# First block in two halves, smaller first weight pieces, an earlier w_out load, and transposes ahead of the first store, in a gated recurrence with a maxout layer

## The chip, the cores and the metric

The kernel runs on one core of a Trainium2 chip. The metric is the device time of one execution in microseconds (us), as the median of several runs. The engines are TensorE (PE; its weight loads are PEld), VectorE (DVE), ScalarE (ACT), GpSimd (POOL) and SyncE (SP). DMAs are issued from SP's and POOL's queues, and two from ACT's at the very end.

## What is computed

The first stage is a gated linear recurrence along the sequence, the second a maxout layer with two weight matrices and an output matrix (4 batches of 6144 positions, 256 features, 1024 hidden):

```
sig = 1 / (1 + exp(-f_logit))
f = lower_bound + (1 - lower_bound) * sig ;  i = 1 - f
for t in range(S):
    h = f[:, t] * h + i[:, t] * x[:, t] ;  y[:, t] = h
h1 = y @ w1 ;  h2 = y @ w2
out = maximum(h1, h2) @ w_out
```

## The kernel before

**Algebra.** With u = sigmoid(-f_logit) the decay is 1 - (1 - lower_bound) * u, and the drive is u * x; the factor (1 - lower_bound) of the drive is left out of the recurrence and put into the weights. As max(h1, h2) = h1 + relu(h2 - h1), the output is y @ (w1 @ w_out) + relu(y @ (w2 - w1)) @ w_out. So the kernel makes `wd` (w2 - w1, scaled, bf16) and `w13` (w1 @ w_out, scaled, bf16) once. `wd` comes from the fp32 difference `wdf`; for `w13` the fp32 w1 is transposed on PE to `w1T`.

**Blocks and chunks.** A block is 512 positions of one batch, 48 in all; features lie on the partitions, in KC = 2 halves of 128. Loads are by chunk: the first four chunks are one block each, the rest two. Chunk 0 is loaded as fp32 by SP and cast by DVE (L95 to L102). Chunks 1 to 3 are loaded with a cast by POOL (L113) and, like chunk 0, turned by PE transposes into PSUM (`turn_steps`, L133). From chunk 4 on POOL casts them into one of two scratch tensors in DRAM (L106), and SP's transposing DMA brings them in (`cross`, L123).

**A block's work.** `gate` (L161): ACT's sigmoid, giving u. `scan_steps` (L175): DVE's drive (v), two decays (ff), two scans (y), each scan starting from the last column of the block before. `first_layer(j, fc)` (L312): for one of FC = 8 hidden blocks, two matmuls with `wd` into the PSUM tile dT (three buffers) and ACT's relu into rt. `second_layer(j, slot)` (L330): the 40 matmuls of the block with w13 and w_out, five a slot, into psO (three buffers); DVE copies psO to osb at L366, SP stores osb at L369 (four osb buffers).

**Order.** The schedule is written by hand: each engine runs its instructions in the order of the text, held only by the data. In the text of the start (L384 to L439) stand: chunk 0's loads, four weight pieces of 512 KB (`fetch_w`, w2 then w1 for each half of the hidden blocks), 8 transposes of an identity, block 0's transposes and recurrence, POOL's wait on the first w1 piece and its load of w_out (L400), a second POOL wait on the second w2 piece, then chunks 1 to 5. Then `turn_w1` (eight fp32 transposes of w1, L288), `make_wd` in steps of two hidden blocks (one DVE subtraction and two ACT scalings each), block 0's first layers in between, `keep_w1T` (copies to w1T, L295), `make_w13`, then block 1's transposes and recurrence, block 0's second layer, block 2's transposes, block 1's first layer, block 2's recurrence, block 3's transposes and gate. A loop over j from 2 then runs first_layer(j) and second_layer(j - 1) side by side, one slot of each in turn, and block j + 1's scan steps among them; for j = 2 all of second_layer(1) comes first. `ahead` issues crossings and fetches a set number of blocks early; in SP's queue the first store stands ahead of the first crossing.

Of the kernel before, what the change touches and what calls it, by code (L numbers as in the profile page):

```python
# [9 lines left out]
FP32 = mybir.dt.float32  # L10
# [8 lines left out]
def kernel(  # L19
# [34 lines left out]
    NCHUNK = len(chunks)  # L54

    def by_xbar(c, s):
        return c >= (4, 4)[s]

    const = ctx.enter_context(tc.tile_pool(name="const", bufs=1))
    wpool = ctx.enter_context(tc.tile_pool(name="wpool", bufs=1))  # L60
# [30 lines left out]
    def fetch(c):  # L91
        b, t0, nt, _ = chunks[c]
        for s in range(2):
            src = srcs[s][b, t0 : t0 + nt, :]
            if c == 0:  # L95
                raw = const.tile([P, nt // P, D], FP32, name=("f0", "x0")[s])
                nc.sync.dma_start(  # L97
                    out=raw[:], in_=src.rearrange("(p i) d -> p i d", p=P)
                )
                nat = natpool.tile([P, CH // P, D], BF16, name=("fn", "xn")[s])  # L100
                nc.vector.tensor_copy(out=nat[:, 0 : nt // P, :], in_=raw[:])  # L101
                held[c, s] = nat  # L102
            elif by_xbar(c, s):
                scr = scratch[s][uses[s] % NSCR]
                uses[s] += 1
                nc.gpsimd.dma_start(  # L106
                    out=scr[0:nt, :].rearrange("(p i) d -> p (i d)", p=P),
                    in_=src.rearrange("(p i) d -> p (i d)", p=P),
                )
                held[c, s] = scr  # L110
            else:
                nat = natpool.tile([P, CH // P, D], BF16, name=("fn", "xn")[s])
                nc.gpsimd.dma_start(  # L113
                    out=nat[:, 0 : nt // P, :].rearrange(
                        "p (k i) d -> p k (i d)", i=TB // P
                    ),
                    in_=src.rearrange(
                        "(k p i) d -> p k (i d)", p=P, i=TB // P
                    ),
                )  # L120
                held[c, s] = nat

    def cross(c):  # L123
        nt = chunks[c][2]
# [28 lines left out]
    def turn(steps):  # L153
        for dst, src in steps:
            nc.tensor.transpose(dst, src, ident[:])  # L155
# [5 lines left out]
    def gate(j):  # L161
        nb = blocks[j][2]
        u = midpool.tile([P, KC, TB], BF16, name="u")
        src = turned[j, 0]
        nc.scalar.activation(  # L165
            out=like(u[:, :, 0:nb], src), in_=src, func=AF.Sigmoid, scale=-1.0
        )
        us[j] = u

    def like(t, src):  # L170
        if len(src.shape) == 3:
            return t
        return t.rearrange("p k (m i) -> p k m i", m=P)

    def scan_steps(j):  # L175
        b, t0, nb, c, o = blocks[j]
        u = us[j]
        ff = midpool.tile([P, KC, TB], BF16, name="ff")
        v = midpool.tile([P, KC, TB], BF16, name="v")
        y = ypool.tile([P, KC, TB], BF16, name="y")  # L180
        ys[j] = y

        def decay(h):
            nc.vector.tensor_scalar(  # L184
                out=ff[:, h, 0:nb],
                in0=u[:, h, 0:nb],
                scalar1=nom[:, h : h + 1],
                scalar2=1.0,
                op0=ALU.mult,
                op1=ALU.add,  # L190
            )

        def drive():
            src = turned[j, 1]
            nc.vector.tensor_tensor(  # L195
                out=like(v[:, :, 0:nb], src),
                in0=like(u[:, :, 0:nb], src),
                in1=src,
                op=ALU.mult,
            )  # L200

        def scan(h):
            if t0 == 0:
                init = 0.0
            else:
                pn = blocks[j - 1][2]
                init = ys[j - 1][:, h, pn - 1 : pn]
            nc.vector.tensor_tensor_scan(  # L208
                out=y[:, h, 0:nb],
                data0=ff[:, h, 0:nb],  # L210
                data1=v[:, h, 0:nb],
                initial=init,
                op0=ALU.mult,
                op1=ALU.add,
            )

        return [
            drive,
            lambda: decay(0),
            lambda: decay(1),  # L220
            lambda: scan(0),
            lambda: scan(1),
        ]

    def recurrence(j):
        gate(j)
        for step in scan_steps(j):
            step()
# [19 lines left out]
    def half(w, g):  # L248
        return w[g][:].rearrange("p kc (m q) -> p kc q m", q=NQ)
# [14 lines left out]
    def pool_waits(t):  # L264
        nc.gpsimd.tensor_copy(out=waited[:], in_=t)

    def pair(w, k):
        return w[:, :, 2 * k * P : 2 * k * P + 2 * P].rearrange(
            "p kc (q m) -> p kc q m", q=2
        )  # L270

    def make_wd(k):
        g, r = divmod(k, NQ // 2)
        qs = slice(2 * r, 2 * r + 2)
        nc.vector.tensor_tensor(  # L275
            out=pair(wdf, k), in0=half(w2n, g)[:, :, qs], in1=half(w1n, g)[:, :, qs],
            op=ALU.subtract,
        )
        cols = slice(2 * k * P, 2 * k * P + 2 * P)
        for kc in range(KC):  # L280
            nc.scalar.mul(wd[:, kc, cols], wdf[:, kc, cols], om[:, kc : kc + 1])  # L281

    def turn_w1(k):
        g, r = divmod(k, NQ // 2)
# [98 lines left out]
    with tc.manual_schedule():  # L383
        nc.sync.dma_start(out=lbc[:], in_=lower_bound.rearrange("(h p) -> p h", p=P))  # L384
        nc.vector.tensor_copy(out=ident[:], in_=ident_f[:])
        nc.vector.tensor_scalar(
            out=om[:], in0=lbc[:], scalar1=-1.0, scalar2=1.0, op0=ALU.mult, op1=ALU.add
        )
        nc.vector.tensor_scalar_add(out=nom[:], in0=lbc[:], scalar1=-1.0)
        fetch(0)  # L390
        for g in range(NG):
            fetch_w(g)
        nc.scalar.activation(out=warm[:], in_=om[:, 0:1], func=AF.Sigmoid)
        wt = ps_d.tile([P, TB], BF16, name="dT")
        for q in range(8):
            nc.tensor.transpose(wt[:, 0:P], ident[:], ident[:])
        turn(turn_steps(0))
        recurrence(0)
        pool_waits(w1n[0][:, 0, 0:1])
        nc.gpsimd.dma_start(  # L400
            out=wob[:].rearrange("p (g q) c -> p g (q c)", g=NG),
            in_=moe_w_out.rearrange("(g p q) c -> p g (q c)", g=NG, q=NQ),
        )
        pool_waits(w2n[1][:, 0, 0:1])
        fetch(1)
        fetch(2)
        done["fetch"] = 3
        ahead("fetch", fetch, LEAD_FETCH)
        pts = [turn_w1(0), turn_w1(1)]
        make_wd(0)  # L410
        make_wd(1)
        for fc in range(0, 2):
            first_layer(0, fc)
        keep_w1T(0, pts[0])
        make_wd(2)
        for fc in range(2, 4):
            first_layer(0, fc)
        make_wd(3)
        keep_w1T(1, pts[1])
        pts = [turn_w1(2), turn_w1(3)]  # L420
        for fc in range(4, 6):
            first_layer(0, fc)
        keep_w1T(2, pts[0])
        for fc in range(6, 8):
            first_layer(0, fc)
        keep_w1T(3, pts[1])
        make_w13()
        turn(turn_steps(1))
        recurrence(1)
        for fc in range(FC):  # L430
            second_layer(0, fc)
        turn(turn_steps(2))
        gate(2)
        for fc in range(FC):
            first_layer(1, fc)
        for step in scan_steps(2):
            step()
        turn(turn_steps(3))
        gate(3)  # L439
        for j in range(2, NBLK + 1):  # L440
            ahead("cross", cross, j + LEAD_CROSS)
            ahead("fetch", fetch, j + LEAD_FETCH)
            steps = turn_steps(j + 2) if j + 2 < NBLK else []
            gates = {}
            if j + 1 < NBLK and by_xbar(blocks[j + 1][3], 0):
                gates[0] = j + 1
            if j + 2 < NBLK and not by_xbar(blocks[j + 2][3], 0):
                gates[FC // 2] = j + 2
            scans = []
            if j == 2:  # L450
                for fc in range(FC):
                    second_layer(1, fc)
            for fc in range(FC):
                if j < NBLK:
                    first_layer(j, fc)
                if j > 2:
                    second_layer(j - 1, fc)
                n = len(steps)
                turn(steps[fc * n // FC : (fc + 1) * n // FC])
                if fc in gates:  # L460
                    gate(gates[fc])
                if fc == 0 and j + 1 < NBLK:
                    scans = scan_steps(j + 1)
                if fc < len(scans):
                    scans[fc]()
# [30 lines left out]
```

## Time and profile before

| | us |
|---|---|
| median of 3 runs | 403.2 (403.06 to 403.27) |
| the profiled execution's own time | 402.93 |
| its span, first to last instruction | 401.1 |
| PE busy | 386.0 (96%) |
| DVE busy | 247.5 (62%) |
| ACT busy | 269.5 (67%) |
| first matmul of the first layer (block 0) | 13.47 |
| last matmul of w13 starts | 21.2 |

The span leaves out some 1.8 us around the first and last instruction. PE's clock is shown as granted in full throughout. A busy share is an average over the span: PE's idle time lies almost wholly in the first 14 us and in one place near 41 us. In a line of the timeline stand the start, the length, the engine, the line of the kernel, the operation, the output and inputs by name, the count, and in brackets the idle time before it and what ended it.

### The profile page before, as it was taken

The page shows a single profiled execution, that of the slowest core. Times are in us where ns is not written, and L with a number is a line of the kernel's source. Part 1 is how long each engine was busy: PE and PEld are TensorE (multiplying, and loading weights), DVE is VectorE, ACT ScalarE, POOL GpSimd, SP SyncE. Part 2 cuts the span into 40 slices and gives each one's busy share as a digit, 9 for nine tenths or more (in the row PEclk, how much of TensorE's full clock was granted, in tenths as well). Part 3 has the DMA queues.
Part 4 walks back from the last instruction along what each step waited for, and adds up shares of the span by engine and source line. Part 5 has one row for each costly group of instructions (what it writes and reads, how often), then busy time and mean ns, then how long its engine had stood idle before and what let it go on. Part 6 is the DMA issues. An engine that isn't in the chain of part 4 may idle for free.

```text
span 401.1 us, 6980 instructions
## 1 busy us (share of the span) xinstructions
PE 386.0 (96%) x2744; PEld 295.1 (74%) x2792; DVE 247.5 (62%) x349; ACT 269.5 (67%) x446; POOL 27.6 (7%) x59
## 2 busy tenths in 40 slices
PE   3899999999999999999999999999999999999996
PEld 2587677777777777777777777777777777777775
DVE  3866656656765665676567566656756665675641
ACT  2656676677667667766766776676667667666762
POOL 0700010010010000000000010000000000000000
PEclk9999999999999999999999999999999999999999
DMA  7999999799999799799899997997995998963212
GB/s 252 208 221 172 247 217 259 170 196 213 223 197 212 205 201 223 171 197 212 203 167 223 195 260 172 191 218 190 217 219 167 177 232 197 181 119 92 106 52 106
DMA packets 103088, 77.00 MB, mean 192 GB/s; under 512 B 93520, under 2 KB 94032, under 8 KB 102352
## 3 DMA queue, kind: packets, MB, share of 16 engines
q1 hardware_dynamic: 100224, 51.13, 52.1%
q0 software_dynamic: 2544, 25.17, 36.8%
q8 instruction: 22, 0.36, 0.4%
q10 hardware_dynamic: 288, 0.26, 0.2%
q14 instruction: 10, 0.08, 0.1%
HBM read 53.48 MB, written 48.23 MB: 254 GB/s over the span
## 4 chain that ended last, share of the span: by engine, by line
PE 94%; DVE 3%; DMA 1%; issue 1%; SPq 0%; ACT 0%; DVEq 0%
PE psO L346 54%; PE dT L317 39%; DMA x_124<-in_x_dram 1%; DVE y L208 1%; PE tT L155 1%; DVE v L195 1%; PE psO L301 0%; DVE ff L184 0%; DVE wdf L275 0%; PE psO L288 0%; DVE xn L101 0%; DVE osb L366 0%; ACT wd L281 0%; SPq L384 0%; SPq L97 0%
## 5 line engine op out<-in xcount | busy, mean ns | idle before, releaser
L325 ACT ACTIVATE rt<-dT 128x512 bf16<-128x512 f32 x384 | 222.1, 598 | 109.5 <-PE dT L317 109.4
L346 PE MATMUL psO<-wob,rt 128*128 128x256 bf16 x1536 | 228.5, 273 | 2.4
L317 PE MATMUL dT<-y,wd 128*128 128x512 bf16 x720 | 217.8, 382 | 2.4 <-ACT wd L281 1.4
L346 PEld LDWEIGHTS <-rt 128*128 128x128 bf16 x1536 | 169.8, 113 | 39.9
L366 DVE COPY osb<-psO 128x512 f32<-128x512 f32 x94 | 64.9, 691 | 75.4 <-PE psO L346 75.4
L208 DVE TENSOR_TENSOR_SCAN y<-ff,y,v 128x512 bf16<-128x512 bf16 x88 | 107.8, 1267 | 0.0
L317 PEld LDWEIGHTS <-wd 128*128 128x128 bf16 x768 | 75.1, 98 | 12.6 <-issue 2.7
L346 PE MATMUL psO<-w_109,y 128*128 128x256 bf16 x384 | 73.3, 273 | 0.0
L346 PEld LDWEIGHTS <-y 128*128 128x128 bf16 x384 | 43.1, 113 | 40.9 <-issue 1.1
L195 DVE TENSOR_TENSOR v<-u,xT 128x1024 bf16<-128x1024 bf16 x44 | 30.5, 692 | 61.2 <-ACT u L165 61.2
L165 ACT ACTIVATE u<-fT 128x1024 bf16<-128x1024 bf16 x44 | 46.2, 1050 | 0.0
L184 DVE TENSOR_SCALAR ff<-u,nom 128x512 bf16<-128x512 bf16 x96 | 29.2, 347 | 0.0
L106 POOL DMA_DIRECT2D scr_0_90<-in_f_logit_dram x11 | 5.4, 493 | 137.0 <-DMA fT<-scr_0_90 137.0
L106 POOL DMA_DIRECT2D scr_1_91<-in_f_logit_dram x11 | 5.5, 496 | 128.2 <-DMA fT<-scr_1_91 127.5
L208 DVE TENSOR_TENSOR_SCAN y<-ff,v 128x512 bf16<-128x512 bf16 x8 | 9.3, 1207 | 0.0
L165 ACT ACTIVATE u<-tT 128x1024 bf16<-128x1024 bf16 x4 | 4.2, 1049 | 7.5 <-PE tT L155 7.5
L195 DVE TENSOR_TENSOR v<-u,tT 128x1024 bf16<-128x1024 bf16 x4 | 4.9, 1218 | 5.4 <-ACT u L165 4.2
L281 ACT ACTIVATE wd<-wdf,om 128x256 bf16<-128x256 f32 x8 | 3.6, 502 | 5.4 <-DVE wdf L275 5.3
L106 POOL DMA_DIRECT2D scr_1_93<-in_x_dram x11 | 5.6, 511 | 16.1 <-DMA xT<-scr_1_93 15.3
L106 POOL DMA_DIRECT2D scr_0_92<-in_x_dram x11 | 5.4, 488 | 14.7 <-DMA xT<-scr_0_92 13.9
L155 PE MATMUL tT<-ident,fn 128*128 128x128 bf16 x32 | 2.9, 242 | 2.8 <-DVE fn L101 2.8
L155 PEld LDWEIGHTS <-fn 128*128 128x128 bf16 x32 | 2.4, 108 | 3.4 <-DVE fn L101 3.1
(34 smaller groups left out, 35.2 us busy)
## 6 DMA issues: line engine op xcount, KB each, us to landing
out_dram<-osb SPq DMA_DIRECT2D x47, 512.0 KB, 3.6
scr_0_90<-in_f_logit_dram POOLq DMA_DIRECT2D x11, 512.0 KB, 6.6
scr_0_92<-in_x_dram POOLq DMA_DIRECT2D x11, 512.0 KB, 8.4
scr_1_91<-in_f_logit_dram POOLq DMA_DIRECT2D x11, 512.0 KB, 6.5
scr_1_93<-in_x_dram POOLq DMA_DIRECT2D x11, 512.0 KB, 8.1
fn<-in_f_logit_dram POOLq DMA_DIRECT2D x3, 256.0 KB, 6.9
xn<-in_x_dram POOLq DMA_DIRECT2D x3, 256.0 KB, 7.6
f_120<-in_f_logit_dram SPq DMA_DIRECT2D x1, 512.0 KB, 3.5
```

Of the source, the lines that this page charges most:

```text
L106: nc.gpsimd.dma_start(out=scr[0:nt, :].rearrange("(p i) d -> p (i d)", p=P), in_=src.rearrange("(p i) d -> p (i d)", p=P),)
L155: nc.tensor.transpose(dst, src, ident[:])
L165: nc.scalar.activation(out=like(u[:, :, 0:nb], src), in_=src, func=AF.Sigmoid, scale=-1.0)
L184: nc.vector.tensor_scalar(out=ff[:, h, 0:nb], in0=u[:, h, 0:nb], scalar1=nom[:, h : h + 1], scalar2=1.0, op0=ALU.mult, op1=ALU.add,)
L195: nc.vector.tensor_tensor(out=like(v[:, :, 0:nb], src), in0=like(u[:, :, 0:nb], src), in1=src, op=ALU.mult,)
L208: nc.vector.tensor_tensor_scan(out=y[:, h, 0:nb], data0=ff[:, h, 0:nb], data1=v[:, h, 0:nb], initial=init, op0=ALU.mult, op1=ALU.add,)
L281: nc.scalar.mul(wd[:, kc, cols], wdf[:, kc, cols], om[:, kc : kc + 1])
L317: nc.tensor.matmul(dT[:, 0:nb], lhsT=wd[:, kc, fc * P : (fc + 1) * P], rhs=y[:, kc, 0:nb], start=(kc == 0), stop=(kc == KC - 1),)
L325: nc.scalar.activation(out=rt[:, 0:nb], in_=dT[:, 0:nb], func=AF.Relu)
L346: nc.tensor.matmul(ps[:, r, :], lhsT=left, rhs=right, start=(s == 0 and (r == 0 or j == NBLK - 1)), stop=(s == n - 1 and (r == 1 or j == N ...
L366: nc.vector.tensor_copy(out=osb[:, 2 * g : 2 * g + 2, :], in_=ps[:])
```

## The change

- Block 0's f and x come in two pieces each of 256 positions (256 KB), in the order f, x, f, x, before the weights. The first half is cast by DVE, the second by ACT. Each half is turned, gated, and run through the recurrence by itself, the second from the last column of the first.
- `make_wd` takes a first hidden block and a count: 0, 1, (2, 3), (4, 5), (6, 7). The scalings of the last four are on DVE in place of ACT.
- POOL waits for the first w2 piece, then loads w_out; its second wait is gone, and chunks 1 to 4 follow. Chunk 5 is fetched at the start of the loop. In the text all of this stands ahead of block 0's work.
- Block 0's first layers come in the order two, both w1T copies, two, then all of the last four after the second `turn_w1` pair.
- The first crossing (chunk 4) is issued ahead of block 0's store in SP's queue.
- In `scan_steps` the two decays come ahead of the drive. Block 3's steps are put between the slots of second_layer(1).

Its core:

```diff
+    def fetch_first(k):
+        nt = TB // 2
+        for s in range(2):
+            raw = const.tile([P, nt // P, D], FP32, name=f"raw{k}{s}")
+            nc.sync.dma_start(
+                out=raw[:],
+                in_=srcs[s][0, k * nt : (k + 1) * nt, :].rearrange(
+                    "(p i) d -> p i d", p=P
+                ),
+            )
+            raws[k, s] = raw
+    def first_bf16(k, s, copy):
+        raw = raws[k, s]
+        nat = const.tile([P, raw.shape[1], D], BF16, name=f"nat{k}{s}")
+        copy(out=nat[:], in_=raw[:])
+        raws[k, s] = nat
+    def first_turn(k):
...
+            dst = ps_t.tile([P, KC, nt // P, P], BF16, name="tT")
+            for q in range(nt // P):
+                for h in range(KC):
+                    nc.tensor.transpose(
...
+    def first_recurrence(k):
...
+        nc.scalar.activation(
+            out=like(u[:, :, cols], fT), in_=fT, func=AF.Sigmoid, scale=-1.0
+        )
+        for h in range(KC):
+            nc.vector.tensor_scalar(
...
+        nc.vector.tensor_tensor(
+            out=like(v[:, :, cols], xT), in0=like(u[:, :, cols], xT), in1=xT,
+            op=ALU.mult,
+        )
+        for h in range(KC):
+            nc.vector.tensor_tensor_scan(
...
+                initial=y[:, h, nt - 1 : nt] if k else 0.0,
...
         return [
-            drive,
             lambda: decay(0),
             lambda: decay(1),
+            drive,
             lambda: scan(0),
             lambda: scan(1),
         ]
...
-    def make_wd(k):
+    def make_wd(fc, n):
...
         for kc in range(KC):
-            nc.scalar.mul(wd[:, kc, cols], wdf[:, kc, cols], om[:, kc : kc + 1])
+            if g == 0:
+                nc.scalar.mul(wd[:, kc, cols], wdf[:, kc, cols], om[:, kc : kc + 1])
+            else:
+                nc.vector.tensor_scalar_mul(
+                    out=wd[:, kc, cols], in0=wdf[:, kc, cols], scalar1=om[:, kc : kc + 1]
+                )
...
-        fetch(0)
+        fetch_first(0)
+        fetch_first(1)
         for g in range(NG):
             fetch_w(g)
+        pool_waits(w2n[0][:, 0, 0:1])
+        nc.gpsimd.dma_start(
+            out=wob[:].rearrange("p (g q) c -> p g (q c)", g=NG),
+            in_=moe_w_out.rearrange("(g p q) c -> p g (q c)", g=NG, q=NQ),
+        )
+        done["fetch"] = done["cross"] = 1
+        ahead("fetch", fetch, 4)
         nc.scalar.activation(out=warm[:], in_=om[:, 0:1], func=AF.Sigmoid)
         wt = ps_d.tile([P, TB], BF16, name="dT")
         for q in range(8):
             nc.tensor.transpose(wt[:, 0:P], ident[:], ident[:])
-        turn(turn_steps(0))
-        recurrence(0)
-        pool_waits(w1n[0][:, 0, 0:1])
...
-        pool_waits(w2n[1][:, 0, 0:1])
-        fetch(1)
-        fetch(2)
-        done["fetch"] = 3
-        ahead("fetch", fetch, LEAD_FETCH)
+        first_bf16(0, 0, nc.vector.tensor_copy)
+        first_bf16(0, 1, nc.vector.tensor_copy)
+        first_turn(0)
+        first_recurrence(0)
+        first_bf16(1, 0, nc.scalar.copy)
+        first_bf16(1, 1, nc.scalar.copy)
+        first_turn(1)
+        first_recurrence(1)
+        for fc in range(2):
+            make_wd(fc, 1)
+        make_wd(2, 2)
         pts = [turn_w1(0), turn_w1(1)]
-        make_wd(0)
-        make_wd(1)
-        for fc in range(0, 2):
+        for fc in range(2):
             first_layer(0, fc)
-        keep_w1T(0, pts[0])
-        make_wd(2)
+        for k in range(2):
+            keep_w1T(k, pts[k])
         for fc in range(2, 4):
             first_layer(0, fc)
-        make_wd(3)
-        keep_w1T(1, pts[1])
+        make_wd(4, 2)
+        make_wd(6, 2)
         pts = [turn_w1(2), turn_w1(3)]
-        for fc in range(4, 6):
+        for fc in range(4, 8):
             first_layer(0, fc)
-        keep_w1T(2, pts[0])
-        for fc in range(6, 8):
-            first_layer(0, fc)
-        keep_w1T(3, pts[1])
+        for k in range(2):
+            keep_w1T(2 + k, pts[k])
         make_w13()
         turn(turn_steps(1))
         recurrence(1)
+        ahead("cross", cross, 4)
...
             if j == 2:
+                if 0 in gates:
+                    gate(gates.pop(0))
+                early = scan_steps(j + 1)
                 for fc in range(FC):
                     second_layer(1, fc)
+                    if fc < 4:
+                        early[fc]()
+                early[4]()
...
-                if fc == 0 and j + 1 < NBLK:
+                if fc == 0 and 2 < j < NBLK - 1:
                     scans = scan_steps(j + 1)
```

## The prediction

> **What bounds the kernel now.** I read the chain of waits first, to see which engine sets the end. It gives TensorE (PE) nearly all of the span, so only time in which PE waits, or does its work slowly, is to be had.
>
> ```profile
> PE 94%; DVE 3%; DMA 1%; issue 1%; SPq 0%; ACT 0%; DVEq 0%
> ```
>
> Then the list of waits, for the places where PE itself is kept (columns: who waits, for whom, us in total, times, longest). From 41.5 us to the end the same list has 0.8 us for PE, and that one wait begins before 41.5.
>
> ```profile
> PE psO L288 <- DMA w1n_110<-in_moe_w_dram: 2.3, 1, 2.3
> PE dT L317 <- ACT wd L281: 1.4, 1, 1.4
> PE dT L317 <- DVE y L208: 0.8, 1, 0.8
> ```
>
> So the change is decided in two places: the start, and one wait of 0.78 us near 41 us. Next the timeline of the start (start, length, engine, line, what).
>
> ```profile
> 5.51 1.03 PE L155 MATMUL tT<-ident,fn 128*128 128x128 bf16 x8 [2.84 <-DVE fn L101]
> ...
> 9.59 2.33 DVE L208 TENSOR_TENSOR_SCAN y<-ff,v 128x512 bf16<-128x512 bf16 x2
> ...
> 10.09 1.96 PE L288 MATMUL psO<-ident_f,w1n_110 128*128 128x128 f32 x8 [2.28 <-DMA w1n_110<-in_moe_w_dram]
> ...
> 11.84 2.02 DVE L275 TENSOR_TENSOR wdf<-w2n_112,w1n_110 128x512 f32<-128x512 f32 x2
> ...
> 13.47 3.60 PE L317 MATMUL dT<-y,wd 128*128 128x512 bf16 x8 [1.42 <-ACT wd L281]
> ...
> 16.86 1.16 PE L288 MATMUL psO<-ident_f,w1n_111 128*128 128x128 f32 x8
> ...
> 19.58 1.91 PE L301 MATMUL psO<-wob,w1T 128*128 128x256 bf16 x16
> ```
>
> The scans of block 0 end at 11.92, only then does VectorE (DVE) begin wd, and PE starts the first layer at 13.47, though w1 had been there since 10. Eight matmuls of the first layer take 3.60 there; later 16 take 3.94. The same eight fp32 transposes of L288 take 1.96 and then 1.16. Instruction by instruction the step falls at 17.0: 0.427 us a matmul of 512 columns before it, 0.216 after; 0.213 and 0.121 for an fp32 transpose. PE runs at half pace until then.
>
> Last, the place of the wait, and the transfers (KB each, us from issue to landing).
>
> ```profile
> 36.51 4.19 PE L317 MATMUL dT<-y,wd 128*128 128x512 bf16 x16
> 36.71 0.69 DVE L366 COPY osb<-psO 128x512 f32<-128x512 f32 x1 [1.49 <-PE psO L346]
> 37.32 1.21 DVE L195 TENSOR_TENSOR v<-u,tT 128x1024 bf16<-128x1024 bf16 x1
> ...
> 38.98 2.45 DVE L208 TENSOR_TENSOR_SCAN y<-ff,y,v 128x512 bf16<-128x512 bf16 x2
> ...
> 41.48 0.38 PE L317 MATMUL dT<-y,wd 128*128 128x512 bf16 x1 [0.78 <-DVE y L208]
> ```
> ```profile
> f_120<-in_f_logit_dram SPq DMA_DIRECT2D x1, 512.0 KB, 3.5
> x_124<-in_x_dram SPq DMA_DIRECT2D x1, 512.0 KB, 4.3
> w2n_112<-in_moe_w_dram SPq DMA_DIRECT2D x1, 512.0 KB, 6.4
> w1n_110<-in_moe_w_dram SPq DMA_DIRECT2D x1, 512.0 KB, 7.3
> ```
>
> DVE had nothing to do from 32.5 to 34.5, with u of block 3 ready at 33.2, yet block 3's steps stand behind both copies of block 1's output.
>
> **What the Trainium skill says.** "TensorE: Matmul & The Clock Gate", Part 1 (the HAM clock gate): PE starts at half clock and gets the full one after about 3.4 us of sustained work, counted in a free-running window of 3.413 us. The trace agrees: first-layer work runs from 13.47, the pace doubles at 17.0. Part 4 of that page (PE-mode transpose) says that transposes don't engage the gate as matmuls do. Here 1.7 us of fp32 transposes from 10.1 and a gap of 1.4 did not bring the step on, which fits, but doesn't prove it. "DMA: Bandwidth & Descriptors", Queues, rings and completion order: each DMA engine takes turns between queues by packets; so a GpSimd load started earlier can take turns from SP's. No run here shows the two overlap for long: the weights land by 12.6, and the first GpSimd load flows from about 13. "VectorE: DVE Perf Modes", on the trn2 errata: a measured fixed term of some 150 cycles an instruction. I use it as an estimate (0.16 us) for halves of instructions the trace has whole.
>
> **The change, part by part.**
>
> *Loads.* f and x of block 0 come as four 256 KB pieces for two of 512, in order f, x, f, x. The 1 KB load took 2.2 from issue, so f's 512 KB took 1.3 of its 3.5; half, issued at 1.26, lands at 1.26+2.2+0.65 = 4.1. The other bound: rows of a piece are 2 KB now, as the weights' are, and the first weight piece took 2.6 after x (6.05 to 8.62) where 1.3 is usual; at that pace 4.8. I take 4.3, x 4.9, the second pair 5.7 and 6.3. The weights have the same bytes before them, and SP's two more issues (0.45 each) are ahead of the data; w1n_110 stays at 10.0 (bounds 9.0, if the slow stretch merges with the ramp, and 11.3, one more slow stretch of 1.3).
>
> *Block 0 in halves.* Cast of 512 elements on DVE: 0.16 + (0.69-0.16)/2 = 0.42, to 4.7. Four transposes: 0.6, to 5.35. Sigmoid on ScalarE (ACT): 0.60 (L325 has that shape), to 6.0. DVE: two decays of 256 at about 0.2 each, drive half of the 1.14 from start to start, 0.6, and two scans of 0.63 (half of 1.25): 0.4+0.6+1.25 = 2.25, to 8.25. The second half's casts are on ACT (0.6 and 0.55, to 7.15), and its sigmoid ends at 7.9, so DVE never waits: 8.25+2.25 = 10.5 for y, against 11.92. Ten small instructions more cost DVE some 1 us in fixed terms, counted in that.
>
> *wd in finer pieces.* wdf of one column block: half of 1.0 and a little, 0.55, to 11.05; its two ACT scalings of 128 columns at 0.36 to 0.4: wd(0) at 11.85. PE's transposes L288 queue ahead and begin at 10.09 as now; the last lets go at 10.09+8*0.213 = 11.8. First layer starts at **11.95**, 1.5 earlier. Next wd(1) at 12.5, wd(2,3) at 13.55: PE wants the latter at 13.66. DVE goes on: two wdf, two w1T copies of 0.65, to 13.85; wd(4,5) on DVE 1.0+0.5 to 15.4; wd(6,7) to 16.9; copies to 18.15. The second half's scalings are on DVE in place of ACT: fp32 of 256, bounds 0.2 and 0.35 (L184), taken 0.25 each, and ACT's four of 0.5 go, hidden as ACT then only has the relus (0.515 apart).
>
> *PE from there.* (a) If PE is at full pace at about 13.6 (transposes count, or a part-filled window is enough): first layers to 14.6, eight fp32 transposes at 0.121 to 15.55, then to 16.4, wait for wd(6) to 16.9, to 17.8; w13's 16 matmuls at 0.109 to 19.55, now 21.33: **1.8 gained**. (b) If 3.4 us of first-layer work are needed: full pace at 15.4; 15.37, 16.35, 18.1, 19.85: 1.5 gained. (c) If the step stays at 17.0: 15.37, transposes at 0.213 to 17.0, 18.75, 20.5: 0.8 gained.
>
> *w_out's cast sooner.* GpSimd (POOL) waits for w2n_112 (8.62) in place of w1n_110 (9.96), and its second wait goes: w_out and then fn, xn and the scratch loads move 1.4 to 1.6 up (w_out from 16.1 to about 14.7, wanted at 17.8; fn of block 1 17.35 to 15.9, wanted at 19.6). Gain nothing: were they not moved, fn at 17.35 and xn at 18.6 would still be there before PE asks, so their price is 0 unless PE comes 1 us sooner than (a). Fetch of chunk 5 is later in the text, but stands in the same place in POOL's queue, so it costs 0.
>
> *Transposes ahead of the first store on SP.* They wait for the scratch loads (now landed 27.7, then 26.3), begin about 2.5 sooner, and the first store queues behind both (11 us now: 8.36 and 3.05). Four output buffers cover it; block 4, whose second layer starts near 55, is the first to need one back. Without that cover a store late by 12 us would cost PE directly. Cost 0.
>
> *Block 3's steps between the second layers of block 1.* decay, decay, drive (0.6+1.2) fit in from 33.2; copy at 35; scan, copy, scan end near 38.6, and PE wants y at 40.7. The 0.78 goes; ACT's relus (41.2) are next, with no room lost. The same reordering elsewhere (decay ahead of drive) has the same sum: 0. Block 1's y keeps its 0.33 us of slack (27.15 against 27.48), as both sides move together.
>
> **Sum.** Start 1.5 to 1.8, wait 0.78: 2.3 to 2.6, middle 2.4. The profiled execution is 402.93 (span 401.1 and 1.8 around it), so 400.5; it lies 0.27 under the runs' median of 403.2, and 403.2-2.4 = **400.8** for the median.
>
> **Rivals.** *The clock step stays* (c): the earlier start is spent at half pace. For it: Part 4, and a fixed window. Against: PE is then busy from 10.1 on without a gap. 0.8+0.78: 401.6. *Only the wait goes:* 2 KB rows load slowly twice, w1n_110 lands at 11.3, the first layer starts at 13.3, the start gains 0.1 at most: 402.3 to 402.4. *Slower:* GpSimd's earlier loads take w1n_111's turns. It lands at 12.6 and DVE wants it at 13.85, so 1.2 are free, and from about 3.8 us of delay on the total is lost. w_out took 2.5 of transfer (13.6 to 16.1), fn and xn 1.25 each: all three ahead of it make 5.0, landing 17.6; wd(4..7) then 17.6+3.05 = 20.65, copies and the end of w13 about 23.2, 1.9 late, less 0.78: 404.3. Against: SP's data is nearly through when POOL's begins.
>
> **Chances.** Forecast (a, b) 0.55; clock step stays 0.25; only the wait 0.11; slower 0.06; better than 400.0 0.03. What the runs can tell from no change is 0.2%, 0.8 us. Faster: 0.55+0.25+0.03 and some of the third, 0.85; same 0.09; slower 0.06. The range takes in (c) with 0.5 for its landings: 400.0 to 402.1.
>
> **What would show it.** First layer of block 0 at 11.95 (before 11.3 or after 12.8: loads misjudged); y of block 0 at 10.5; the 512-column pitch of 0.216 from 13.6 or 15.4; w13 done by 19.6 to 19.9; no wait for y at L317 near 38; fn of block 1 ahead of PE. A PE wait for w1n_111 or fn, or for wd(6) over 1 us, would break the sum.

## The result, and the profile after

The first four executions of the changed kernel gave a ratio of 0.9939 to the kernel before (95% interval 0.9915 to 0.9963). Some executions run 8 to 190 us longer (two of these four, 423.0 and 430.1 us; 26 of 68 of the changed kernel's variants below, 2 of 26 of the kernel before's variants, none of its own 69): medians and ratios leave them out, their profiles are read only up to w13, and whether the change makes them likelier was not tried. A later set of five, beside the kernel before on the same chip:

| | us |
|---|---|
| changed kernel, 5 executions | 400.77 (400.67 to 401.20) |
| kernel before, 17 executions there | 403.76 (402.89 to 404.21) |
| ratio | 0.9931 (0.9919 to 0.9943) |
| span of the profiled executions | 398.9 after, 401.1 before |

The forecast was 400.8, from a gain of 2.4. That the median meets it to 0.03 is in part luck: on this chip the kernel before stands at 403.76 and not at 403.2, and the ratio makes the gain 2.8 (2.3 to 3.3; the first set's makes it 2.5, 1.5 to 3.4). The profile shown here is that of the later set; its trace leaves buffer numbers out of the names. The chain of waits has nothing but PE in it behind the first weights:

```profile
PE 96%; DMA 2%; SPq 1%; issue 0%; DVE 0%
```

In the list of waits up to 42 us PE waits for w1 as it did, but no longer for wd, and not for y:

```profile
PE tT L141 <- DVE nat L132: 2.4, 2, 1.9
PE psO L352 <- DMA w1n<-in_moe_w_dram: 2.3, 1, 2.3
...
PE dT L468 <- DVE ident L449: 1.6, 1, 1.6
```

PE's timeline of the start (start, length, engine, line, what):

```profile
10.38 1.95 PE L352 MATMUL psO<-ident_f,w1n 128*128 128x128 f32 x8 [2.27 <-DMA w1n<-in_moe_w_dram]
12.13 3.51 PE L381 MATMUL dT<-y,wd 128*128 128x512 bf16 x8
15.48 1.11 PE L352 MATMUL psO<-ident_f,w1n 128*128 128x128 f32 x8
16.43 1.89 PE L381 MATMUL dT<-y,wd 128*128 128x512 bf16 x8
18.15 1.91 PE L365 MATMUL psO<-wob,w1T 128*128 128x256 bf16 x16
```

The first layer starts at 12.13 where it started at 13.47, straight behind the transposes of w1. The pace doubles at 15.40 (the second eight matmuls take half as long as the first), and w13 starts at 18.15 for 19.58: **1.43 gained at the start**. Not every execution gets as much. In the profile of the first set (the execution of 430.1 us) the first w1 piece landed at 11.05, the pace doubled at 17.11, and w13 started only 0.23 sooner than in the kernel before:

```profile
11.18 1.95 PE L352 MATMUL psO<-ident_f,w1n_110 128*128 128x128 f32 x8 [3.44 <-DMA w1n_110<-in_moe_w_dram]
12.93 3.62 PE L381 MATMUL dT<-y,wd 128*128 128x512 bf16 x8
...
19.35 1.91 PE L365 MATMUL psO<-wob,w1T 128*128 128x256 bf16 x16
```

VectorE in the later set's profile:

```profile
9.34 1.39 DVE L278 TENSOR_TENSOR_SCAN y<-ff,y,v 128x256 bf16<-128x256 bf16 x2
10.65 2.13 DVE L333 TENSOR_TENSOR wdf<-w2n,w1n 128x256 f32<-128x256 f32 x3
...
13.89 1.07 DVE L333 TENSOR_TENSOR wdf<-w2n,w1n 128x512 f32<-128x512 f32 x1
15.00 0.61 DVE L343 TENSOR_SCALAR wd<-wdf,om 128x256 bf16<-128x256 f32 x2
15.53 1.15 DVE L333 TENSOR_TENSOR wdf<-w2n,w1n 128x512 f32<-128x512 f32 x1
16.71 0.61 DVE L343 TENSOR_SCALAR wd<-wdf,om 128x256 bf16<-128x256 f32 x2
```

y of block 0 ends at 10.73 for 11.92, and VectorE then works without a gap until wd(6,7) at 17.32, 6.59 behind y. In the kernel before wd(6,7) is complete at 18.55, 6.63 behind y:

```profile
17.64 0.91 ACT L281 ACTIVATE wd<-wdf,om 128x256 bf16<-128x256 f32 x2
```

So the new order of wd, its scalings and the w1T copies left this distance as it was, and y's earlier end is what moved: 1.23 of the 1.43 are wd(6,7) coming sooner, and the other 0.20 are PE, which starts w13 0.83 behind it for 1.03. The other place, near 36 us:

```profile
33.42 0.69 DVE L430 COPY osb<-psO 128x512 f32<-128x512 f32 x1
34.02 1.28 DVE L233 TENSOR_TENSOR_SCAN y<-ff,y,v 128x512 bf16<-128x512 bf16 x1
35.28 0.69 DVE L430 COPY osb<-psO 128x512 f32<-128x512 f32 x1
35.89 1.27 DVE L233 TENSOR_TENSOR_SCAN y<-ff,y,v 128x512 bf16<-128x512 bf16 x1
```
```profile
35.08 4.32 PE L381 MATMUL dT<-y,wd 128*128 128x512 bf16 x18
39.24 0.38 PE L410 MATMUL psO<-w,y 128*128 128x256 bf16 x2
```

Block 3's y is done at 37.16, over 1.5 us ahead of its first use, and no wait is left. From the start of block 2's first layer to the start of its second layer it was 36.51 to 41.70, now 35.08 to 39.24: **1.03 gained**. The starts of block 3's first two matmuls show where, before and after:

```profile
40.31 0.39 PE L317 MATMUL dT<-y,wd 128*128 128x512 bf16 x1
41.48 0.38 PE L317 MATMUL dT<-y,wd 128*128 128x512 bf16 x1 [0.78 <-DVE y L208]
```
```profile
38.81 0.59 PE L381 MATMUL dT<-y,wd 128*128 128x512 bf16 x2
```

Now the two start 0.216 apart. Before, each stood behind one of the two scans of y, which end at 40.25 and 41.43, and they started 1.17 apart. That is 0.95 of the 1.03, and the first of them came 0.07 late as well. The idle time of 0.78 is counted only from the modelled end of the matmul at 40.31, which is 40.70. So the whole 1.03 is the wait for y, and 0.78 was too small a reading of it. The last matmul starts at 394.96 for 397.42: 2.46, which is 1.43 + 1.03. The spans differ by 2.18, as what follows the last matmul took 0.28 longer. The transfers of the start (KB each, median us from issue to landing):

```profile
w2n<-in_moe_w_dram SPq DMA_DIRECT2D x2, 512.0 KB, 6.6
w1n<-in_moe_w_dram SPq DMA_DIRECT2D x2, 512.0 KB, 7.4
...
raw<-in_f_logit_dram SPq DMA_DIRECT2D x2, 256.0 KB, 3.4
raw<-in_x_dram SPq DMA_DIRECT2D x2, 256.0 KB, 3.8
```

The four pieces landed at 4.03, 5.19, 6.18 and 6.81, the first w1 piece at 10.25.

### The profile page after: what moved, and what is told of

It reads as the page before. It is cut to its first block, busy times and chain, and to the rows that moved or that the text cites. A ratio compares the mean times of both kernels' runs of the same rounds, so it can differ in the third digit from the quotient of the medians.

```text
span 428.3 us, 6970 instructions
## 1 busy us (share of the span) xinstructions
PE 392.8 (92%) x2744; PEld 296.8 (69%) x2792; DVE 248.7 (58%) x359; ACT 268.5 (63%) x447; POOL 26.4 (6%) x58
## 4 chain that ended last, share of the span: by engine, by line
PE 46%; DMA 34%; SPq 15%; ACT 3%; DVE 1%; issue 1%; ACTq 0%
PE psO L410 25%; DMA fT<-scr_0_90 20%; PE dT L381 19%; SPq L153 13%; DMA fT<-scr_1_91 12%; ACT u L190 2%; DMA w1n_110<-in_moe_w_dram 2%; SPq L433 1%; PE psO L352 1%; ACT rt L389 1%; PE tT L180 1%; PE psO L365 0%; SPq L121 0%; DVE osb L430 0%; DVE y L233 0%
## 5 line engine op out<-in xcount | busy, mean ns | idle before, releaser
L389 ACT ACTIVATE rt<-dT 128x512 bf16<-128x512 f32 x384 | 219.2, 598 | 104.1 <-PE dT L381 100.0
L233 DVE TENSOR_TENSOR_SCAN y<-ff,v 128x512 bf16<-128x512 bf16 x6 | 7.0, 1208 | 0.0
L98 POOL DMA_DIRECT2D scr_0_92<-in_x_dram x11 | 5.4, 488 | 18.7 <-DMA xT<-scr_0_92 16.9
L190 ACT ACTIVATE u<-tT 128x1024 bf16<-128x1024 bf16 x3 | 3.2, 1058 | 4.3 <-PE tT L180 4.3
L352 PE MATMUL psO<-ident_f,w1n_110 128*128 128x128 f32 x8 | 1.9, 422 | 3.4 <-DMA w1n_110<-in_moe_w_dram 3.4
L341 ACT ACTIVATE wd<-wdf,om 128x128 bf16<-128x128 f32 (+1 forms) x6 | 2.2, 428 | 4.3 <-DVE wdf L333 4.3
L352 PEld LDWEIGHTS psO<-ident_f,w1n_110 128*128 128x128 f32 x8 | 1.6, 221 | 3.7 <-issue 3.7
L220 DVE TENSOR_TENSOR v<-u,tT 128x1024 bf16<-128x1024 bf16 x3 | 3.6, 1216 | 0.0
```

What stands on the lines that cost most here:

```text
L98: nc.gpsimd.dma_start(out=scr[0:nt, :].rearrange("(p i) d -> p (i d)", p=P), in_=src.rearrange("(p i) d -> p (i d)", p=P),)
L190: nc.scalar.activation(out=like(u[:, :, 0:nb], fT), in_=fT, func=AF.Sigmoid, scale=-1.0)
L220: nc.vector.tensor_tensor(out=like(v[:, :, 0:nb], xT), in0=like(u[:, :, 0:nb], xT), in1=xT, op=ALU.mult,)
L233: nc.vector.tensor_tensor_scan(out=y[:, h, 0:nb], data0=ff[:, h, 0:nb], data1=v[:, h, 0:nb], initial=init, op0=ALU.mult, op1=ALU.add,)
L352: nc.tensor.transpose(pt[:, kc, q, :], half(w1n, g)[:, kc, 2 * r + q], ident_f[:])
L389: nc.scalar.activation(out=rt[:, 0:nb], in_=dT[:, 0:nb], func=AF.Relu)
```

## The experiments

Each was timed beside the kernel before on the same chip; ratios are to that.

**The changed kernel again.** No edit.

> The changed kernel as it is, to get its trace beside the kernel before. Theory (two gains: an earlier first layer, worth 0.8 to 1.8 us, and no wait for block 3's y, 0.78 us): 400.6 to 401.6 us, PE at the first layer of block 3 some 1.6 to 2.6 us ahead of the kernel before, and the same distance at the end. Rival (the clock step decides: it stays at 17.0 us after the start of the program whatever PE does before): the distance ahead of block 1's first layer is 0.2 to 0.8 us only, 1.0 to 1.6 us after block 3, and what is left of the measured gain comes from later in the program.

400.77, ratio 0.9931, as shown. Block 3's first layer comes 2.46 us ahead by its second matmul, so both gains are there. Against the rival the step fell at 15.40, not at 17.0; but in the first set's profile it fell at 17.11, and the rival was right that the step isn't tied to the first layer (see the clock below).

**The wait alone**, on the kernel before:

```diff
         return [
-            drive,
             lambda: decay(0),
             lambda: decay(1),
+            drive,
...
             if j == 2:
+                early = scan_steps(j + 1)
                 for fc in range(FC):
                     second_layer(1, fc)
+                    if fc < 4:
+                        early[fc]()
+                early[4]()
...
-                if fc == 0 and j + 1 < NBLK:
+                if fc == 0 and 2 < j < NBLK - 1:
```

> The kernel before with one edit: block 3's steps between the slots of block 1's second layer (and decay ahead of drive). Theory: the 0.78 us wait for y goes and nothing else moves: 402.4 us, 0.8 under the kernel before. Rival (the wait is only handed on, to the relus or to block 4's y): 403.0 to 403.3 us.

402.38 (12 executions), ratio 0.9973 (0.9964 to 0.9982), so 0.7 to 1.5 us gained. In its trace the stretch from block 2's first to second layer is 37.16 to 41.32, 4.16 long like the changed kernel's. The wait is not handed on: the first theory holds, with a gain of 1.03 in this stretch for its 0.78.

**First crossing behind the first store again**, in the changed kernel:

```diff
-        ahead("cross", cross, 4)
```

> The changed kernel with the first crossing behind the first store again in SP's queue. Theory: the order of the two on SP costs and brings nothing, so the same time as the changed kernel within 0.2 us. Rival (the earlier transposes are what brings the part of the gain that the start doesn't show, as block 4 no longer comes late): 0.5 to 1 us slower than the changed kernel.

400.73 (400.60 to 401.36), ratio 0.9933 (0.9920 to 0.9946). No difference from the changed kernel: the medians are 0.04 apart, and in the profiles the last matmul starts at 394.87 for 394.96.

**GpSimd's old waits**, in the changed kernel:

```diff
-        pool_waits(w2n[0][:, 0, 0:1])
+        pool_waits(w1n[0][:, 0, 0:1])
...
+        pool_waits(w2n[1][:, 0, 0:1])
         done["fetch"] = done["cross"] = 1
```

> The changed kernel with the GpSimd waits of the kernel before (w_out after the first w1 piece, the other loads after the third weight piece). Theory: w_out and block 1's inputs still land before PE asks, so the same time as the changed kernel within 0.2 us. Rival (an earlier w_out was needed, PE comes to w13 or to block 1's transposes before the loads): 0.5 to 1.5 us slower. Other rival (the earlier loads take turns from the weight pieces): up to 0.5 us faster, with the second w1 piece landing earlier than in the changed kernel.

400.87 (400.83 to 400.89, three executions), ratio 0.9931 (0.9917 to 0.9946). Neither rival: w13 starts at 18.05 without a wait for w_out, and the weights did not come sooner (the second w1 piece at 13.07 for 12.90).

**Fill of matmuls**, in the changed kernel:

```diff
-        wt = ps_d.tile([P, TB], BF16, name="dT")
-        for q in range(8):
-            nc.tensor.transpose(wt[:, 0:P], ident[:], ident[:])
+        wt = ps_d.tile([P, TB], FP32, name="dT")
+
+        def fill(n):
+            for q in range(n):
+                nc.tensor.matmul(
+                    wt[:, 0:P], lhsT=ident[:], rhs=ident[:], start=True, stop=True
+                )
+
+        fill(26)
...
         first_turn(0)
+        fill(4)
...
         first_turn(1)
+        fill(24)
```

> The changed kernel with 54 matmuls of 128 columns on the identity (nobody reads their result) in PE's gaps before the first weights: 26 in place of the 8 first transposes, 4 and 24 behind the two halves' transposes. Theory (the full pace comes at the end of the first window of 3.41 us that is filled well enough with PE work, and the window's start differs from run to run): the pace doubles before 10.4 us in every run, the fp32 transposes of w1 take 1.0 us for 1.95, the first layer starts at 12.0 as wd(0) is not there earlier, and then VectorE's chain is late: wd(6) at 17.1 to 17.3, w13 from about 18.0. So 400.5 to 400.7 us, the best executions of the changed kernel, with less spread. Rival (PE's half pace is still what sets the end of the start): w13 from 17.0, 399.6 us.

400.38 and 400.64, two executions, too few for an interval. PE's timeline:

```profile
1.62 2.95 PE L470 MATMUL dT<-ident 128*128 128x128 bf16 x26 [1.62 <-DVE ident L449]
...
10.14 1.20 PE L352 MATMUL psO<-ident_f,w1n 128*128 128x128 f32 x8 [1.14 <-DMA w1n<-in_moe_w_dram]
11.59 1.27 PE L381 MATMUL dT<-y,wd 128*128 128x512 bf16 x4 [0.25 <-ACT wd L341]
13.22 1.47 PE L381 MATMUL dT<-y,wd 128*128 128x512 bf16 x4 [0.36 <-ACT wd L341]
...
16.92 1.08 PE L381 MATMUL dT<-y,wd 128*128 128x512 bf16 x4 [0.41 <-DVE wd L343]
17.84 1.91 PE L365 MATMUL psO<-wob,w1T 128*128 128x256 bf16 x16
```

Full pace from 4.5 us on, and PE now waits for wd at each step (0.25, 0.36, 0.41). w13 starts at 17.84, only 0.3 us sooner than without the fill, and not at 17.0: once PE is fast, VectorE's chain to wd(6) is the end of the start.

**Fill of transposes.** The same with the transposes kept.

> The same fill as 54 bf16 transposes of the identity instead of matmuls. If transposes count towards the full pace like matmuls: the same as the fill with matmuls, with the step before 10.4 us. If they don't, as the Trainium skill's page on TensorE (PE-mode transpose) has it: the step comes only after first-layer work has filled a window, at 15.4 to 18.8 us, w13 from 18.1 to 20, 400.6 to 402 us.

400.64 (three executions), ratio 0.9931 (0.9916 to 0.9945). The pace doubled at 9.21, before any matmul of the first layer, so these transposes count.

**Block 0 whole**, in the changed kernel (the first edit in all three functions of block 0):

```diff
-        nt = TB // 2
+        nt = TB
...
-        fetch_first(1)
...
-        first_bf16(1, 0, nc.scalar.copy)
-        first_bf16(1, 1, nc.scalar.copy)
-        first_turn(1)
-        first_recurrence(1)
```

> The changed kernel with block 0 whole: f and x in one piece each, casts on VectorE, one gate, one recurrence; all else as changed. Theory: y of block 0 is done at 11.8 for 10.7, wdf of the first hidden block follows, wd(0) at 13.1, the first layer starts at 13.2 for 12.1, and w13 and the end come 0.8 to 1.1 us later: 401.6 to 401.9 us. Rival (w1's landing at 10.3 and its transposes set the start, not y): within 0.3 us of the changed kernel.

Ratio 0.9977 (0.9956 to 0.9998; four executions, 401.19 to 404.18), so 401.6 to 403.3 us: slower than the changed kernel, by 1.9 between the ratios and by 0.5 between the near ends of their intervals. y ends at 11.85, wd(0) at 13.08, the first theory's chain to 0.1, and w13 starts at 19.32, 1.17 later than in the changed kernel.

**Coarser wd**, in the changed kernel:

```diff
-        for fc in range(2):
-            make_wd(fc, 1)
+        make_wd(0, 2)
         make_wd(2, 2)
```

> The changed kernel with the first two hidden blocks of wd made in one piece again (one subtraction of 512, two scalings of 256). Theory: wd(0) is complete at 12.7 for 12.0, so the first layer starts at 12.75, 0.6 later, and VectorE's chain is 0.1 us shorter: 0 to 0.6 us slower than the changed kernel, 401.0 us. Rival (PE is held by its own transposes until 12.1 and then by the pace, so finer pieces bring nothing): within 0.1 us.

400.84 (400.43 to 401.39), ratio 0.9939 (0.9927 to 0.9951): no difference that can be told, and both forecasts lie within it. In the profile PE starts later, but w13 doesn't:

```profile
12.65 2.94 PE L381 MATMUL dT<-y,wd 128*128 128x512 bf16 x8
...
18.18 1.91 PE L365 MATMUL psO<-wob,w1T 128*128 128x256 bf16 x16
```

The first layer is 0.52 later, but it starts straight behind the transposes of w1, which landed 0.52 later in this execution (10.77 for 10.25); so this profile doesn't show what the coarser piece costs there. w13 is 0.03 later: wd(6,7) is complete at 17.46 for 17.32, and w13 starts 0.72 behind it.

**Whole loads, halves behind them**, in the changed kernel:

```diff
-            raw = const.tile([P, nt // P, D], FP32, name=f"raw{k}{s}")
+            raw = const.tile([P, 2, nt // P, D], FP32, name=f"raw{k}{s}")
...
+            for h in range(2):
+                raws[h, s] = raw[:, h]
...
-        fetch_first(1)
```

> The changed kernel with f and x of block 0 loaded in one piece each again, but cast, turned, gated and run through the recurrence in halves as changed. Theory (the halves pay because half of f and x is there sooner): x lands at 6.0 for 5.2, the first half's drive waits for it, y of block 0 ends at 11.4 for 10.7, and all behind it on VectorE with it: 401.3 to 401.5 us. Rival (the halves pay as VectorE, ScalarE and PE overlap within the block, whenever the data lands): y by 10.9, within 0.2 us of the changed kernel.

401.36 (401.23 to 406.88, eleven executions), ratio 0.9958 (0.9940 to 0.9976). The first theory's time holds and the rival is out. y ends at 11.70 (11.4 foretold): behind whole loads, working in halves brings y forward by 0.15 (from 11.85), and the other 0.97 (to 10.73) come only with loading in pieces. Loading in pieces without working in pieces was not tried.

**The fill alone**, on the kernel before (26 and 24 matmuls):

> The kernel before with the fill of 128-column matmuls alone (26 in place of the first 8 transposes, 24 behind block 0's transposes). Theory (PE's half pace is only in part what sets the start, VectorE's chain is next): the first layer starts at 13.4 as before, the pace doubles before 10.4, wd(6) stays at 18.1 to 18.5 and w13 starts at about 19.0 for 19.6: 402.7 us, less spread than the kernel before. Rival (the half pace is all that holds the start of the kernel before): w13 from 18.1, 401.7 us.

402.96 (402.44 to 405.02), ratio 0.9989 (0.9978 to 1.0001): at most 0.9 us faster, and perhaps no faster at all; the forecast of 402.7 lies within that, but the trace is neither theory's. The pace doubled at 10.93, about as foretold, but fell back at 14.35 and came again at 17.76, and w13 started at 19.69. The windows view (stretch; its length; PE busy and its matmuls; granted clock; DMA share and GB/s) has it. Ahead of the first change on record, here 10.93, it prints 1.00 although the matmuls run at half pace:

```profile
7.52:10.93 3.41, 3.41 (x30) 1.00 1.05 399
10.93:14.35 3.42, 1.62 (x11) 1.00 0.87 172
14.35:17.76 3.41, 3.41 (x13) 0.50 1.11 202
```

In the middle stretch PE was kept for 1.79 us by wd, and the clock was taken back to 0.50 for the next.

**Fill, and the crossing behind the store.**

> The changed kernel with the fill of matmuls and with the first crossing behind the first store again. Theory: as the fill alone, 400.5 us within 0.2: the place of the crossing costs and brings nothing. Rival (with PE ahead the earlier crossing is needed): 0.3 to 1 us slower than the fill alone.

400.76 (400.44 to 401.20, four executions), ratio 0.9930 (0.9917 to 0.9943). With the fill's two executions at 400.5 no difference can be told. In this profile the pace doubled at 4.40, fell back at 7.82 and came again at 11.23, so the fill doesn't hold the full pace in every execution; w13 started at 18.00 all the same.

**The second w1T copy later.** As the last one, and:

```diff
-        for k in range(2):
-            keep_w1T(k, pts[k])
+        keep_w1T(0, pts[0])
...
         make_wd(6, 2)
+        keep_w1T(1, pts[1])
```

> As the last one, and the second w1T copy stands behind the last wd pieces on VectorE. Theory (with PE at full pace, VectorE's chain up to wd(6) sets the start): wd(6) at 16.5 for 17.1, w13 from 17.3 but held up to 0.4 us by the last copies, so 0.2 to 0.6 us faster than the fill: 400.0 to 400.3 us. Rival (ScalarE's relus or w13's other inputs are next at once): 400.5 us as before.

400.80 (400.42 to 400.93), ratio 0.9929 (0.9917 to 0.9940): a miss. wd(6,7) is complete at 16.89 and w13 does start sooner, but stands still in its middle:

```profile
16.27 0.62 DVE L343 TENSOR_SCALAR wd<-wdf,om 128x256 bf16<-128x256 f32 x2
...
16.81 1.88 DVE L359 CAST w1T<-psO 128x512 bf16<-128x512 f32 x3
...
17.61 0.93 PE L365 MATMUL psO<-wob,w1T 128*128 128x256 bf16 x6
...
18.74 1.27 PE L365 MATMUL psO<-wob,w1T 128*128 128x256 bf16 x10 [0.20 <-DVE w1T L359]
```

The order on VectorE moves the wait from wd to w1T; the sum of VectorE's work up to w13 is the bound. To take the last four's scalings (0.61 twice) off VectorE again, back to ScalarE, was not tried. No version tried is measurably faster than the changed kernel.

## Why the prediction was right, and where not

**The sum** was 1.5 to 1.8 for the start and 0.78 for the wait, middle 2.4; measured were 1.43 and 1.03, 2.46 by the last matmul. The start's case (b) was met nearly to the number, step at 15.4 foretold and 15.40 in the trace, 1.5 against 1.43, but that was luck: (b) counts 3.4 us from the start of the first layer, and in this execution a window of the clock happened to open 0.14 ahead of it.

**Loads.** First pair 4.3 and 4.9 foretold, 4.03 and 5.19 found; second 5.7 and 6.3, found 6.18 and 6.81. w1n_110 was to stay at 10.0. In the nine profiles with four pieces it landed at 9.84 to 11.05 (middle one 10.36), in the five with two pieces at 9.80 to 10.13 (middle one 9.87). So the two more pieces cost the weights some 0.5, and up to 1.1 (11.05 for 9.96), which was set at nothing. VectorE, busy with y until 10.7, waited for them long in one profile only (0.46), the first set's. There w1 came close to the bound of 11.3 (a second slow stretch), and the start gained 0.23, so that the rival built on it ("only the wait goes") came near; by the times of both sets it is out.

**Halves.** y at 10.5 foretold, 10.73 found. The halved instructions priced with a fixed term of 0.16 (the Trainium skill, "VectorE: DVE Perf Modes", on the trn2 errata) came out well: the cast 0.43 for 0.42. The drive took 0.69 where the working put 0.6 between starts, and it stood at 0.72 from start to start. ("Some 1 us" for ten more small instructions doesn't follow from that term, which makes 1.6; the sum doesn't use it.)

**wd in finer pieces.** wd(0) 11.98 for 11.85, first layer 12.13 for 11.95, wd(6,7) 17.32 for 16.9. The times hold, the worth doesn't: "1.5 earlier" at the first layer is not where the gain is decided. What the prediction named only in case (a), the wait for wd(6), decides in most profiles: in seven of the changed kernel's variants (all but block 0 whole and whole loads) w13 starts 0.71 or 0.72 behind wd(6,7), though the pace first doubled anywhere between 4.40 and 14.80. Where it doubled later, PE's pace was the last: by 0.1 at 15.40 (0.83 behind wd(6,7)) and by 0.8 at 17.11 (1.54). wd(6,7) in turn comes 6.5 to 6.7 behind y, in block 0 whole as in the changed kernel; it came 7.1 behind where w1 landed at 11.05, and 5.95 with the later w1T copy. So y's earlier end is what pays.

**The clock.** (a), (b) and (c) were put as three mechanisms; they are one with a chance start. With the changed kernel's order on PE all three step times came up, or nearly: a step at 13.57 (w_out late), 15.40 and 17.11 (the first set), with w13 from 18.05, 18.15 and 19.35, where 17.8, 18.1 and 18.75 follow from the prediction. The Trainium skill ("TensorE: Matmul & The Clock Gate", Part 1) has a free-running window of 3.413 us. The trace's clock record agrees: the steps of one execution lie whole multiples of 3.413 apart, and their place against the program differs from run to run. The share of each window that PE spends streaming (columns at the pace of the moment, 128-column fp32 transposes counted twice, as they take twice as long) tells which window ends in full pace. Both shares are of the window:

```
kernel               window          streaming   of it transposes   pace after
before               10.15 - 13.56      51%           48%            half
before               13.56 - 16.97     100%            3%            full
changed, first set   10.28 - 13.70      72%           50%            half
the wait alone       11.80 - 15.22      57%            0%            half
late w1T copy         3.02 -  6.43      72%      (with fill)         half
late w1T copy         6.43 -  9.84      79%      (with fill)         full
fill of matmuls       1.09 -  4.50      80%      (with fill)         full
coarser wd           11.34 - 14.76     100%           38%            full
w_out late           10.16 - 13.57      88%           50%            full
fill of transposes    5.80 -  9.21      91%           91%            full
fill, kernel before   0.69 -  4.11      73%      (fill alone)        half
fill, kernel before  10.93 - 14.35      35%           16%            falls to half
fill, cross behind    4.40 -  7.82      28%      (with fill)         falls to half
fill of matmuls       4.50 -  7.91      43%      (with fill)         stays full
```

So up at 79% and more, not at 73% and less; down at 28% and 35%, not at 43%. "Coarser wd" has 62% of matmuls in its window, less than the 73% of matmuls that failed elsewhere; only with its transposes is it enough. That, and the fill of transposes, decide against the page's Part 4 (PE-mode transpose) for the transposes of these kernels: the measurement has them count. (The trace lists them as MATMUL and doesn't show the mode they ran in.) The prediction took Part 4 as a point for (c), and was wrong there. The step also fell at 18.63 in one profile (the wait alone), 5.36 us after its first matmul, and that execution is 0.65 later at w13 than the kernel before as profiled (20.23 for 19.58). The kernel before as profiled, with its step 3.5 us after the first matmul, was among the lucky ones (402.93, where its 69 executions lie between 402.75 and 404.40); on the chip of the later set its executions spread over 1.3 us (402.89 to 404.21). That this spread is the window's place was not shown for each execution, as few executions were profiled.

**w_out sooner, and the crossing ahead of the store:** 0 foretold, and no difference found for either. The slower rival, w1 behind GpSimd's loads, is out as well: with GpSimd's old waits nothing changes.

**The wait.** 0.78 foretold, 1.03 found. The mechanism was right and the size short, by its reading: "PE wants y at 40.7" takes the modelled end of block 3's first matmul. That matmul started at 40.31, the next would have started at 40.53, 0.216 later, and started at 41.48.

## What to carry to other kernels

An earlier start is worth what the last link of the chain moves, so look for the engine that works without a gap up to the point where the stages join (here VectorE up to wd(6) and w1T), not for the one whose first instruction comes sooner. Where instructions wait in order behind work that isn't urgent (block 3's scans behind two output copies), moving them among it was free here. Size a wait from start to start of the instructions around it: the idle time in the list begins only at a modelled end, and showed 0.78 for 1.03. Smaller first pieces of work pay when the data lands in pieces too: behind whole loads the halves brought y 0.15 forward, with loads in pieces 1.12.

## What the runs showed of the hardware

In these traces TensorE's pace goes up only at the end of a window of 3.413 us in which it streamed 79% or more, transposes included, and it falls back at 35% or less: filling PE early, on the kernel before, was undone by a window with a wait of 1.79 us (10.93 to 14.35). As the window's place is chance, the full pace came 1.3 to 4.8 us after the first layer began in seven profiles of the changed kernel and of its variants without fill (1.3 with w_out late, 4.2 in the first set, 4.8 with whole loads), and 3.5 and 5.4 us after it in the kernel before and the wait alone. Two more pieces ahead in SP's queue, with the same bytes, put the weights some 0.5 us later (middle 10.36 for 9.87), with a spread of 1.2 us over the nine profiles.
